# New orders of the TensorE, ScalarE and VectorE queues in the pair loop of a fused agent-attention and two-FFN kernel, with six of eight second-layer roundings on ScalarE

## Chip, cores and metric

The kernel runs on one NeuronCore of a Trainium2 chip. The metric is device time in microseconds (us), as the median over runs. Three runs of the kernel before took 1089.06, 1089.34 and 1089.91 us. The profiled execution is one further run.

## What is computed

The reference is an agent attention over 12480 tokens of width 128 with 49 agents, followed by two feed-forward layers of inner width 2048:

```python
a2k = sm(agents, k);  agent_v = a2k @ v
q2a = sm(q, agents);  x = q2a @ agent_v          # 12480 x 128
h = x @ w_in                                      # 12480 x 2048
g = where(h >= 1, h, where(h <= -1, 0, (h + 1)**2 / 4))
x = g @ w_out
h = x @ moe2_w_in
g = s * max(h, 0)**2 + b
out = g @ moe2_w_out
```

All of it is fp32. The weights of both layers arrive as 64-bit words and are decoded on the chip.

## The kernel before

A prologue computes `agent_v`, decodes the weights, and folds `agent_v` into the first layer's weights. A hand-written ramp then starts the first steps. From there on the function `steady()` runs to the end, and it is the part that matters here.

The tokens are cut into 25 tiles: the first of 256 columns, then 23 of 512, then one of 448. The inner width is cut into eight steps per tile, each of 256 rows (two blocks of 128), so there are 200 steps per layer. One step of a layer is a chain over the engines. In layer 1, for step n:

- H on TensorE makes the hidden block in PSUM; the two steps of a pair are made together by `H1_pair` (lines 720 and 726). Line 726 uses four quarters of the array at once.
- R and S on ScalarE are the two halves of the activation: a Relu out of PSUM (line 739) and a Square in place (line 745).
- M on VectorE caps the result (line 749) and is the last reader of that PSUM block.
- c on VectorE rounds it to `gh` (line 760), and L subtracts to get the remainder `gl` (line 765).
- O on TensorE multiplies by the output weights in six matmuls (line 804): for each of two blocks `gh` twice, then `gl`. The result is the tile `y`.

Layer 2 has the same chain in small letters: h (line 689, six matmuls), r (line 741), t (line 745), then the rounding, which is g: `G` on ScalarE (line 758) or `C` on VectorE (line 760), then l (line 765) and o (line 804, into the tile `o`). Layer 2 runs 11 steps behind layer 1. When a tile's eight steps are through, Y (line 823) and y (line 826) bring the first layer's result out of PSUM, and Z (line 830) brings out the second layer's as `osb`. The PSUM tiles `y` and `o` have one buffer each, so the first matmul of a tile waits for Y and y, or for Z, of the tile before. The hidden blocks h share three PSUM buffers, handed out in turn; `gh` and `gl` have four buffers per layer, x has three.

For later tiles the attention's softmax runs inside the same loop. Once in eight pairs of steps q (line 261) makes the scores of two tiles, Q (line 269) transposes them on VectorE, and twelve fillers F follow, one or two at a time; the last of them is a `spread` with a 1280-wide transposition (line 284), whose result 32 small DMAs take apart.

What sets the order: each engine works strictly through its own list, and the lists come from three strings in `PAIR`, used once per pair of steps n0, n0+1. A token is a letter and 0 or 1, for the step n0 or n0+1 (the small letters then mean the step 11 behind, or 12 and 13 behind for t, g, l and o). Tokens with nothing to do in a pair are skipped: Y, y and Z come up once in four pairs, q and Q once in eight. Which engine rounds is a pattern over the steps:

```python
def GH(layer, n):
    if layer == 1:
        return PAT1[n] if n < len(PAT1) else "0"
    return PAT2[n % len(PAT2)] if n < NS - TL else "0"
```

A "1" puts the rounding on ScalarE, a "0" on VectorE. The last steps run from the table `TAIL`.

Of the kernel before, what the change touches and what calls it, by code (L numbers as in the profile page):

```python
# [18 lines left out]
def kernel(  # L19
# [29 lines left out]
    Q1, QW, QG = 3, 256, 8  # L49

    GR, XB, UB, WB, KV = 4, 3, 4, 2, 7
    WARM, CD = 10, 1
    PAT1, PAT2, TL = "10011010001001", "11111101", 11

# [31 lines left out]
    PIECE = {"A0": (0, 512), "A2": (512, 512)}  # L88
    NR = 14
    PAIR = {  # L90
        "PE": "H0 h0 O0 o0 O1 h1 q1 o1".split(),
        "ACT": "t0 Y0 R0 R1 S0 S1 G0 r0 Y1 t1 r1 G1".split(),
        "DVE": "L0 y0 C0 C1 Z1 F0 M0 M1 l0 Z0 c0 y1 c1 L1 Q1 l1 F1".split(),
    }
    TAIL = {
        "PE": "H0 O0 h0 o0 O1 h1 o1".split(),
# [890 lines left out]
```

## Time and profile before

| | |
|---|---|
| median of three runs | 1089.34 us |
| the profiled execution's own time | 1089.8 us |
| its span, first to last instruction | 1088.0 us |
| TensorE busy | 1056.8 us, 97% of the span |
| VectorE busy | 961.4 us, 88% |
| ScalarE busy | 981.7 us, 90% |
| mean granted TensorE clock | 0.995 of full speed |

The busy time of an engine is the time that its instructions covered. For TensorE the ends of matmuls are modelled: a row of a matmul carries a duration that overlaps with the matmul after it, so the starts of two matmuls say more than the duration of one. A span of 1088.0 us and a time of 1089.8 us leave 1.8 us outside the profiled instructions. In the rows, PE is TensorE, PEld its weight load, DVE is VectorE, ACT is ScalarE.

### The profile page before, as it was taken

How to read it: one execution, taken by the hardware profiler on the slowest of the kernel's cores; microseconds unless marked ns; L12 is line 12 of the kernel's file. 1: busy time of each engine (PE TensorE's matmuls, PEld its weight loads, DVE VectorE, ACT ScalarE, POOL GpSimd, SP SyncE). 2: the span in 40 equal slices, each digit the busy share in tenths (PEclk: the TensorE clock that was granted, in tenths of full speed). 3: DMA queues.
4: the chain of work that ended last, by engine and by line, in shares of the span. 5: the costliest groups of instructions: out<-in, count | busy, mean ns of one | idle time of the engine just before them, and what ended most of it. 6: DMA issues, size and time to landing. Idle time of an engine off the chain costs nothing.

```text
span 1088.0 us, 13453 instructions
## 1 busy us (share of the span) xinstructions
PE 1056.8 (97%) x4962; PEld 793.3 (73%) x4962; DVE 961.4 (88%) x1114; ACT 981.7 (90%) x1101; POOL 0.9 (0%) x7
## 2 busy tenths in 40 slices
PE   6889989999999999999999999999999999999998
PEld 2667667777777777777777777777777777777777
DVE  8889979988988988988988988989989989988876
ACT  6889779999999999999999999999999999999986
POOL 0000000000000000000000000000000000000000
PEclk9899999999999999999999999999999999999999
DMA  9930020010020020020020020020020010010000
GB/s 349 395 103 29 21 63 10 17 53 10 13 57 11 12 57 11 11 57 10 12 57 10 11 59 10 10 59 10 8 60 11 9 41 11 9 38 10 1 11 19
DMA packets 32130, 47.68 MB, mean 44 GB/s; under 512 B 7301, under 2 KB 23669, under 8 KB 31425
## 3 DMA queue, kind: packets, MB, share of 16 engines
q1 hardware_dynamic: 32065, 46.83, 13.5%
q8 instruction: 39, 0.64, 0.3%
q14 instruction: 26, 0.21, 0.1%
HBM read 27.58 MB, written 6.39 MB: 31 GB/s over the span
## 4 chain that ended last, share of the span: by engine, by line
PE 74%; DVE 9%; ACT 8%; issue 4%; DMA 2%; SPq 2%; DVEq 0%; ACTq 0%
PE h L689 22%; PE o L804 22%; PE y L804 19%; PE h L720 6%; ACT x L739 3%; PE h L726 3%; DVE gl L765 3%; ACT x L745 3%; DVE x L749 2%; DMA wu<-in_w_out 2%; SPq L297 1%; ACT x L741 1%; DVE osb L830 1%; PE qs L261 1%; PE av L546 1%
## 5 line engine op out<-in xcount | busy, mean ns | idle before, releaser
L765 DVE TENSOR_TENSOR gl<-x,gh 128x1024 fp32r<-128x1024 f32 (+2 forms) x399 | 465.9, 1188 | 13.2 <-ACT gh L758 12.2
L745 ACT ACTIVATE x<-x 128x1024 f32<-128x1024 f32 (+2 forms) x399 | 403.2, 1039 | 2.6
L749 DVE SCALAR_TENSOR_TENSOR x<-h,x 128x1024 f32<-128x1024 f32 (+2 forms) x200 | 230.1, 1189 | 88.1 <-ACT x L745 88.0
L741 ACT ACTIVATE x<-h 128x1024 f32<-128x1024 f32 (+2 forms) x199 | 200.4, 1007 | 47.9 <-PE h L689 43.1
L739 ACT ACTIVATE x<-h 128x1024 f32<-128x1024 f32 (+2 forms) x200 | 190.1, 1002 | 18.8 <-PE h L726 16.7
L758 ACT ACTIVATE gh<-x 128x1024 fp32r<-128x1024 f32 (+1 forms) x172 | 176.7, 1029 | 1.1 <-DVE x L749 1.1
L689 PE MATMUL h<-yh,wi2h 128*128 128x512 f32 (+2 forms) x400 | 165.9, 415 | 5.1 <-DVE x L749 3.1
L804 PE MATMUL o<-gh,wo2h 128*128 128x512 f32 (+2 forms) x400 | 159.0, 398 | 3.8 <-DVE osb L830 2.7
L804 PE MATMUL y<-gl,wo1h 128*128 128x512 f32 (+2 forms) x400 | 156.4, 391 | 2.2 <-DVE gl L765 2.2
L804 PE MATMUL o<-gl,wo2h 128*128 128x512 f32 (+2 forms) x400 | 157.4, 393 | 0.6 <-DVE gl L765 0.4
L804 PE MATMUL y<-gh,wo1h 128*128 128x512 f32 (+2 forms) x400 | 155.9, 390 | 0.0
L804 PE MATMUL o<-gh,wo2l 128*128 128x512 f32 (+2 forms) x400 | 155.8, 390 | 0.0
L804 PE MATMUL y<-gh,wo1l 128*128 128x512 f32 (+2 forms) x400 | 155.7, 389 | 0.0
L689 PE MATMUL h<-yh,wi2l 128*128 128x512 f32 (+2 forms) x400 | 155.6, 389 | 0.0
L689 PE MATMUL h<-yl,wi2h 128*128 128x512 f32 (+2 forms) x400 | 155.5, 389 | 0.0
L760 DVE CAST gh<-x 128x1024 fp32r<-128x1024 f32 (+2 forms) x227 | 147.2, 674 | 6.8 <-ACT x L745 6.6
L689 PEld LDWEIGHTS h<-yh,wi2h 128*128 128x128 f32 x400 | 74.9, 187 | 42.8 <-issue 12.3
L720 PE MATMUL h<-pt,awm 128*128 128x512 f32 (+1 forms) x368 | 100.0, 394 | 0.0
L804 PEld LDWEIGHTS o<-gh,wo2h 128*128 128x128 f32 x400 | 75.2, 188 | 32.9 <-ACT x L745 12.0
L804 PEld LDWEIGHTS o<-gl,wo2h 128*128 128x128 f32 x400 | 75.3, 188 | 22.3 <-DVE gl L765 5.4
L804 PEld LDWEIGHTS y<-gl,wo1h 128*128 128x128 f32 x400 | 75.1, 188 | 21.3 <-DVE gl L765 4.5
L804 PEld LDWEIGHTS y<-gh,wo1h 128*128 128x128 f32 x400 | 75.1, 188 | 17.1
(127 smaller groups left out, 837.9 us busy)
## 6 DMA issues: line engine op xcount, KB each, us to landing
k<-in_kT SPq DMA_DIRECT2D x12, 512.0 KB, 11.4
v<-in_v_main SPq DMA_DIRECT2D x12, 512.0 KB, 10.1
out_T<-osb SPq DMA_DIRECT2D x23, 256.0 KB, 2.0
pt<-turned SPq DMA_DIRECT2D x172, 32.0 KB, 1.9
px<-turned SPq DMA_DIRECT2D x172, 32.0 KB, 1.8
qbuf<-in_qT SPq DMA_DIRECT2D x10, 512.0 KB, 3.8
wu<-in_w_in SPq DMA_DIRECT2D x4, 1024.0 KB, 12.0
wu<-in_w_out SPq DMA_DIRECT2D x3, 1024.0 KB
```

The costliest lines, as they stand in the source:

```text
L261: nc.tensor.matmul(out=sc[j * RG:(j + 1) * RG, g], lhsT=a64[:, g * RG:(g + 1) * RG], rhs=qbuf[:, c0:c0 + QW].rearrange("p (b x) -> p b x", ...
L689: nc.tensor.matmul(out=h[:, i, :w], lhsT=a[:, sl], rhs=r, start=(m == 0), stop=(m == len(ops) - 1))
L720: nc.tensor.matmul(out=out[g], lhsT=awm[:, c * P:(c + 1) * P], rhs=pt_t[t][:, :w], start=True, stop=False)
L726: nc.tensor.matmul(out=out[g], lhsT=awx[r, q], rhs=px_t[t][r, :w], start=False, stop=True)
L739: nc.scalar.activation(out=x, in_=h, func=ACTF.Relu, scale=0.5, bias=0.5)
L741: nc.scalar.activation(out=x, in_=h, func=ACTF.Relu)
L745: nc.scalar.activation(out=x, in_=x, func=ACTF.Square)
L749: nc.vector.scalar_tensor_tensor(out=x, in0=h, scalar=1.0, in1=x, op0=ALU.max, op1=ALU.min)
L758: nc.scalar.activation(out=a, in_=x, func=ACTF.Copy)
L760: nc.vector.tensor_copy(out=a, in_=x)
L765: nc.vector.tensor_tensor(out=b, in0=x, in1=a.bitcast(F32), op=ALU.subtract)
L804: nc.tensor.matmul(out=o[:, :w], lhsT=l[:, c, :], rhs=r[:, i, :w], start=(c == 0 and m == 0), stop=(c == KF - 1 and m == 2),)
```

## The change

Three strings and one pattern are replaced. No instruction is new in kind, and no buffer changes. Over the kernel, ScalarE has 24 instructions fewer and VectorE 24 more: the second-layer rounding of the steps with n mod 8 = 2.

```diff
     GR, XB, UB, WB, KV = 4, 3, 4, 2, 7
     WARM, CD = 10, 1
-    PAT1, PAT2, TL = "10011010001001", "11111101", 11
+    PAT1, PAT2, TL = "10011010001001", "11011101", 11
     PIECE = {"A0": (0, 512), "A2": (512, 512)}
     NR = 14
     PAIR = {
-        "PE": "H0 h0 O0 o0 O1 h1 q1 o1".split(),
-        "ACT": "t0 Y0 R0 R1 S0 S1 G0 r0 Y1 t1 r1 G1".split(),
-        "DVE": "L0 y0 C0 C1 Z1 F0 M0 M1 l0 Z0 c0 y1 c1 L1 Q1 l1 F1".split(),
+        "PE": "H0 O0 o0 h0 O1 h1 o1 q1".split(),
+        "ACT": "t0 R0 S0 G0 R1 S1 Y0 r0 Y1 t1 G1 r1".split(),
+        "DVE": "y0 Z1 C0 L0 C1 M0 F0 Z0 l0 c0 M1 y1 L1 l1 c1 Q1 F1".split(),
     }
     TAIL = {
         "PE": "H0 O0 h0 o0 O1 h1 o1".split(),
```

How this moves instructions is shown for one pair, n0 = 116. Names carry the layer and the step (`h1_116`, `gh2_104`, `x2_105`), then a running number; `y14` and `o12` carry the tile.

On TensorE, the first row of each block of the pair, before:

```order
L720 MATMUL h1_116_5537<-pt14_4756,awm_654 128x512 x2
...
L689 MATMUL h2_105_5547<-yh13_5383,wi2h_78 128x512
...
L804 MATMUL y14_5493<-gh1_114_5480,wo1h_76 128x512
...
L804 MATMUL o12_5240<-gh2_103_5530,wo2h_80 128x512
...
L804 MATMUL y14_5493<-gh1_115_5482,wo1h_76 128x512
...
L689 MATMUL h2_106_5596<-yh13_5383,wi2h_78 128x512
...
L804 MATMUL o13_5603<-gh2_104_5578,wo2h_80 128x512
```

and now:

```order
L720 MATMUL h1_116_5537<-pt14_4770,awm_654 128x512 x2
...
L804 MATMUL y14_5426<-gh1_114_5492,wo1h_76 128x512
...
L804 MATMUL o12_5245<-gh2_103_5526,wo2h_80 128x512
...
L689 MATMUL h2_105_5559<-yh13_5382,wi2h_78 128x512
...
L804 MATMUL y14_5426<-gh1_115_5533,wo1h_76 128x512
...
L689 MATMUL h2_106_5600<-yh13_5382,wi2h_78 128x512
...
L804 MATMUL o13_5607<-gh2_104_5575,wo2h_80 128x512
```

The block h0 (`h2_105`) has moved from ahead of both O0 and o0 to behind them, so that between the end of tile `o12` (its last block, on `gh2_103`) and the first block of `o13` there now lie three blocks in place of two. In pairs with q, its eight short matmuls stand behind o1 and no longer ahead of it.

On ScalarE, the pair n0 = 16 (the order is the same in every pair, but this one also has a Y, `yh1`, and the softmax's Exp, `turned`), before:

```order
L745 ACTIVATE x2_4_1105<-x2_4_1105 128x2x256
L306 ACTIVATE turned_653<-turned_653 128x8x49
L739 ACTIVATE x1_16_1155<-h1_16_1120 128x1024
L739 ACTIVATE x1_17_1157<-h1_17_1121 128x1024
L745 ACTIVATE x1_16_1155<-x1_16_1155 128x1024
L745 ACTIVATE x1_17_1157<-x1_17_1157 128x1024
L758 ACTIVATE gh2_4_1161<-x2_4_1105 128x2x256
L741 ACTIVATE x2_5_1163<-h2_5_1130 128x2x256
L823 ACTIVATE yh1_1165<-y1_892 128x512
L745 ACTIVATE x2_5_1163<-x2_5_1163 128x2x256
L741 ACTIVATE x2_6_1203<-h2_6_1180 128x2x256
L758 ACTIVATE gh2_5_1205<-x2_5_1163 128x2x256
```

and now:

```order
L745 ACTIVATE x2_4_1109<-x2_4_1109 128x2x256
L739 ACTIVATE x1_16_1154<-h1_16_1119 128x1024
L745 ACTIVATE x1_16_1154<-x1_16_1154 128x1024
L758 ACTIVATE gh2_4_1157<-x2_4_1109 128x2x256
L739 ACTIVATE x1_17_1159<-h1_17_1120 128x1024
L745 ACTIVATE x1_17_1159<-x1_17_1159 128x1024
L741 ACTIVATE x2_5_1162<-h2_5_1141 128x2x256
L823 ACTIVATE yh1_1164<-y1_892 128x512
L745 ACTIVATE x2_5_1162<-x2_5_1162 128x2x256
L758 ACTIVATE gh2_5_1168<-x2_5_1162 128x2x256
L306 ACTIVATE turned_653<-turned_653 128x8x49
L741 ACTIVATE x2_6_1222<-h2_6_1186 128x2x256
```

Each S now stands right behind the R whose result it reads, the rounding `gh2_4` comes two instructions earlier, and `gh2_5` right behind the Square that feeds it and ahead of the next r. The Exp, which waits for VectorE's softmax steps, stood ahead of this pair's R and now stands behind its G1.

On VectorE, the pair n0 = 116 again, before:

```order
L765 TENSOR_TENSOR gl1_115_5535<-x1_115_5428,gh1_115_5482 128x1024
L749 SCALAR_TENSOR_TENSOR x1_116_5572<-h1_116_5537,x1_116_5572 128x1024
L749 SCALAR_TENSOR_TENSOR x1_117_5574<-h1_117_5538,x1_117_5574 128x1024
L765 TENSOR_TENSOR gl2_104_5585<-x2_104_5528,gh2_104_5578 128x1024
L830 TENSOR_SCALAR osb12_5587<-o12_5240,s_sb_70,bcol_72 128x512
L760 CAST gh1_116_5590<-x1_116_5572 128x1024
L760 CAST gh1_117_5592<-x1_117_5574 128x1024
L765 TENSOR_TENSOR gl1_116_5594<-x1_116_5572,gh1_116_5590 128x1024
L765 TENSOR_TENSOR gl2_105_5633<-x2_105_5580,gh2_105_5622 128x1024
```

and now:

```order
L765 TENSOR_TENSOR gl1_115_5535<-x1_115_5445,gh1_115_5533 128x1024
L749 SCALAR_TENSOR_TENSOR x1_116_5572<-h1_116_5537,x1_116_5572 128x1024
L830 TENSOR_SCALAR osb12_5586<-o12_5245,s_sb_70,bcol_72 128x512
L765 TENSOR_TENSOR gl2_104_5589<-x2_104_5528,gh2_104_5575 128x1024
L760 CAST gh1_116_5591<-x1_116_5572 128x1024
L749 SCALAR_TENSOR_TENSOR x1_117_5577<-h1_117_5538,x1_117_5577 128x1024
L765 TENSOR_TENSOR gl1_116_5594<-x1_116_5572,gh1_116_5591 128x1024
L765 TENSOR_TENSOR gl2_105_5596<-x2_105_5580,gh2_105_5583 128x1024
L760 CAST gh1_117_5598<-x1_117_5577 128x1024
```

The second M (`x1_117`) has moved from right behind the first one to behind `osb`, l0 and c0, and so `osb12` has moved up past that M and past l0. A filler F0, where one is due, stood ahead of both M and now stands between the first M and Z0; the subtraction l1 (`gl2_105`) now precedes c1.

## Rows read from the trace of the kernel before

**Rows 1.** Busy us of each engine (and instructions) from 174.40 to 1011.63 us, clock, DMA.
```profile
174.40:1011.63 837.23, 834.11 (x3754) 625.69 (x3752) 753.33 (x824) 780.80 (x830) 0.00 (x0) 1.00 0.09 25
```

**Rows 2.** Timeline of TensorE: start and duration in us; L720 begins a pair.
```profile
613.61 1.09 PE L720 MATMUL h<-pt,awm 128*128 128x512 f32 x4
...
615.06 0.50 PE L689 MATMUL h<-yh,wi2h 128*128 128x512 f32 x1
...
623.83 1.08 PE L720 MATMUL h<-pt,awm 128*128 128x512 f32 x4
...
634.13 1.08 PE L720 MATMUL h<-pt,awm 128*128 128x512 f32 x4
...
645.28 1.08 PE L720 MATMUL h<-pt,awm 128*128 128x512 f32 x4
...
655.23 0.62 PE L720 MATMUL h<-pt,awm 128*128 128x512 f32 x2
```

**Rows 3.** Timeline of TensorE and VectorE around a first matmul of a tile o.
```profile
631.71 0.80 DVE L830 TENSOR_SCALAR osb<-o,s_sb,bcol 128x512 f32<-128x512 f32 x1
632.15 0.40 PE L689 MATMUL h<-yh,wi2l 128*128 128x512 f32 x1
...
632.66 0.48 PE L804 MATMUL o<-gh,wo2h 128*128 128x512 f32 x1
```

**Rows 4.** Timeline of the same two engines one pair earlier.
```profile
617.87 1.50 DVE L284 STREAM_TRANSPOSE turned<-packed 128x1280 f32<-128x1280 f32 x1
619.29 2.31 DVE L749 SCALAR_TENSOR_TENSOR x<-h,x 128x1024 f32<-128x1024 f32 x2
621.53 1.20 DVE L765 TENSOR_TENSOR gl<-x,gh 128x1024 fp32r<-128x1024 f32 x1
...
622.16 0.40 PE L804 MATMUL o<-gh,wo2h 128*128 128x512 f32 x1
...
622.39 0.39 PE L804 MATMUL o<-gh,wo2l 128*128 128x512 f32 x1
...
622.79 0.50 PE L804 MATMUL o<-gl,wo2h 128*128 128x512 f32 x1
```

**Rows 5.** Timeline of ScalarE in two pairs.
```profile
599.92 1.02 ACT L741 ACTIVATE x<-h 128x1024 f32<-128x1024 f32 x1
600.97 1.06 ACT L745 ACTIVATE x<-x 128x1024 f32<-128x1024 f32 x1
...
603.37 1.05 ACT L758 ACTIVATE gh<-x 128x1024 fp32r<-128x1024 f32 x1
604.32 1.05 ACT L745 ACTIVATE x<-x 128x1024 f32<-128x1024 f32 x1
```

**Rows 6.** Two of the page's costliest groups: busy us, mean ns of one.
```profile
L758 ACT ACTIVATE gh<-x 128x1024 fp32r<-128x1024 f32 (+1 forms) x172 | 176.7, 1029 | 1.1 <-DVE x L749 1.1
...
L760 DVE CAST gh<-x 128x1024 fp32r<-128x1024 f32 (+2 forms) x227 | 147.2, 674 | 6.8 <-ACT x L745 6.6
```

**Rows 7.** Timeline of two early pairs, n0 = 16 and n0 = 24, each to the next.
```profile
109.87 1.09 PE L720 MATMUL h<-pt,awm 128*128 128x512 f32 x4
...
113.48 0.55 ACT L306 ACTIVATE turned<-turned 128x392 f32<-128x392 f32 x1 [3.49 <-DVE turned L303]
...
118.10 0.39 PE L689 MATMUL h<-yh,wi2h 128*128 128x256 f32 x1 [1.81 <-DVE x L749]
...
120.85 1.80 PE L720 MATMUL h<-pt,awm 128*128 128x512 f32 x4
...
152.33 1.08 PE L720 MATMUL h<-pt,awm 128*128 128x512 f32 x4
...
156.53 0.54 ACT L306 ACTIVATE turned<-turned 128x392 f32<-128x392 f32 x1 [3.69 <-DVE turned L303]
...
164.45 1.08 PE L720 MATMUL h<-pt,awm 128*128 128x512 f32 x4
```

**Rows 8.** Busy us and granted clock (the first number after POOL's) of a short stretch.
```profile
118.90:122.50 3.60, 3.25 (x12) 2.29 (x10) 3.60 (x6) 2.37 (x5) 0.00 (x0) 0.53 0.00 0
```

## The prediction

> **What bounds the kernel now.** I read the stretch table first, because the page's average mixes a prologue with the loop. Between the first matmul of pair n0 = 28 (174.40 us) and that of n0 = 192 (1011.63 us) lie 82 pairs in 837.23 us, and TensorE is busy for 834.11 of them; ScalarE is busy 93% of the stretch, VectorE 90% [rows 1]. Read so, TensorE is full and there is nothing to win. The timeline says otherwise. Two matmuls of one block start 0.23 us apart, while each row claims 0.39 to 0.40 us [rows 4]: a row covers its successor's start, so a gap of up to 0.16 us does not show as idle. The measure to use is the time from one pair's first matmul to the next one's. It is 9.95 us in a pair with no wait (645.28 to 655.23). This is also the sum of its parts: H takes 1.45 (613.61 to 615.06), then six blocks of six matmuls at 0.23 make 8.4, and 0.1 is left for the change from quarter-array to full matmuls [rows 2, 4]. The other three pairs shown take 10.22, 10.30 and 11.15 us [rows 2]. The last one holds the eight score matmuls q, so q costs 1.20.
>
> The 10.30 is a wait for `osb`: a matmul due 0.23 after 632.15 starts at 632.66, because `osb` began at 631.71 and took 0.80 [rows 3]. The 10.22 is a wait for `gl`: the third matmul of an o block starts 0.40 after the second, when the subtraction that began at 621.53 has ended. That subtraction had stood behind the spread's transposition (1.50) and two caps (2.31) [rows 4]. So TensorE is the bound, and it loses time only where VectorE delivers late.
>
> A rule bears on this. The page Perfetto Trace Analysis of the Trainium skill (Identifying the Most-Contended Engine) says that the busy share of matmuls does not measure how near TensorE is to its limit. The trace agrees: by busy share 3.1 us of the stretch could be won, by start times three times that.
>
> **Term 1, the loop from n0 = 28 to 192.** With no wait left it would take 82 x 9.95 + 9 x 1.20 (nine pairs with q) = 826.7 us against 837.23: a gain of 10.5. Counted by waits: a tile ends in 21 of the pairs, at 0.35, and the spread falls in 10, at 0.27, together 10.1, so these two waits are the whole loss. The question is whether the new queues remove them and bring no other. I walk one pair by hand, from its first matmul at 0.
>
> TensorE: H 0, O0 1.45, o0 2.95, h0 4.35, O1 5.75, h1 7.15, o1 8.55, next pair 9.95.
>
> ScalarE: an instruction that reads its predecessor's result starts 0.03 after that one's end, so 1.05 after its start (599.92 to 600.97); one that doesn't starts 0.95 after it (603.37 to 604.32) [rows 5]. The new order makes R-S (twice), r0-t1 and r1-t0 pairs of the dear kind, and t1-G1 as well (1.09). With R0 at 1.65 (H's last matmuls end shortly after the next block begins): S0 2.70, G0 3.65, R1 4.60, S1 5.65, r0 6.60, t1 7.65, G1 8.74, r1 9.69, t0 10.74, R0 11.69. That is 10.04 per pair with G0 and 9.09 without. Half the pairs now have none, so the mean is 9.57; Y in one pair of four and the Exp in one of eight add about 0.2 (estimate: each half of a full instruction). ScalarE thus needs some 9.75 of 9.95: it fits, with 0.2 to spare.
>
> VectorE: M0 waits for S0, 2.70 + 1.06 + 0.03 = 3.79, and takes 1.16. `osb` follows directly: 4.95 to 5.75. The first matmul of the next tile wants it at 8.55; there were 0.1 to 0.3 too few, now there are 2.8 to spare. Then l0 6.95, c0 7.63, M1 8.79, L1 10.0, l1 11.2 (G1 is there at 9.82), c1 11.9, next L0 13.1, each time being an end. They are wanted: l0 at 9.02 (third matmul of o1), M1 at 9.95 (its PSUM buffer for the next H), c0 at 11.40, L1 at 11.87, l1 at 13.37. The least margin is 1.2, M1 before H. In the pair with the spread, 1.50 replaces `osb`: l0 ends at 7.65, which is 1.4 in time where it was late. M1 then ends at 9.5, and that pair also has a C0 in front (0.67), so M1 beats H by 0.4 at best. This spot I price from 0 to 0.4 us, ten times: 0 to 4.
>
> Moving 24 roundings costs VectorE 24 x 0.67 = 16 us and frees ScalarE of 24 x 1.03 = 25 [rows 6]. Both lie beside TensorE's work, VectorE going from 90 to about 92% of the stretch; without that cover the 16 would be on the path. I take 10.5 for the term. No wait is left to win beyond it, so that is its upper end; the lower end is a loss, which rival 3 prices.
>
> **Term 2, two early pairs.** Pair 16 takes 10.98 us (109.87 to 120.85) and pair 24 takes 12.12 (152.33 to 164.45). In both, ScalarE stands 3.49 and 3.69 us at the softmax's Exp, which waits for VectorE, with both R queued behind it; then h waits for a cap, 1.81 us at 118.10 [rows 7]. Now the Exp stands behind G1, at the end of a pair, and R0 starts when H is ready. In pair 16 four blocks work on the 256-column tile, 24 matmuls at half of 0.23, so TensorE needs only 7.2. ScalarE needs 2 x (1.05 + 0.95) for R and S, about 3.3 for six half-width instructions and 0.9 for Y and Exp, so 8.2, and that bounds it: a gain of 2.8. Pair 24 should come to 10.1, as h0, which shares its PSUM buffer with the softmax's scores, now stands 2.9 us later: a gain of 2.0. Together 4.8, with ends 0 (the stall returns at another instruction) and 7 (the neighbours gain too). For the pairs between and the end of the program I add 0.5.
>
> Part of pair 16's loss is the clock. From 118.90 to 122.50 the granted clock was 0.53 of full speed, mostly 1.2 GHz and not 2.4, right after the idle of 1.81 us [rows 7, 8]; (1 - 0.53) x 3.60 = 1.7 us. That it falls after idling is what the page TensorE: Matmul & The Clock Gate (HAM oscillation) says, and by it a shorter idle keeps the clock. The 2.8 counts this already.
>
> **Sum.** 1089.8 - 10.5 - 4.8 - 0.5 = 1074.0 for an execution like the profiled one; that one lay 0.46 above the median of 1089.34, so 1073.5.
>
> **Rivals.**
> 1. *Nothing to win.* TensorE's busy share is the truth and its starts are paced by something that no queue order moves: at most the 3.1 us of idle go [rows 1], so 1086 to 1089. Against it: the pair without a wait takes 9.95 and the ones with a named wait more.
> 2. *Half of it.* The thin spot (M1 before H after the spread) takes up to 4, or the early stall only changes place, with VectorE's transposition of the scores still waiting for the 32 DMAs: 1078 to 1086. For it: those DMAs aren't touched. Against: a margin of 0.4, and only pairs 22 to 24 are near the DMAs.
> 3. *Slower: ScalarE becomes the bound.* Place: the ring t0 to r1 in each pair. It fits by 0.2 us, and the new order puts five instructions behind their own producer. If each of these cost 0.04 more than rows 5 say, ScalarE paces the loop, and every further 0.1 per pair adds about 9 us over 90 pairs. It undoes the whole gain of 15.8 at 0.18 per pair beyond the fit, so 0.4 in all, 4% of the ring; at 6%, 1107 us. For it: ScalarE is already busy 93% [rows 1]. Against: the same R-S spacing of 1.05 is in the trace now, between r0 and t1.
> 4. *The change doesn't do what it says.* The order lists show 24 instructions changing sides and the blocks moved, so I give this nothing.
>
> **How the numbers follow.** The forecast (1070 to 1078) has 0.74, rival 2 has 0.15, rival 1 has 0.05, rival 3 has 0.06. The range from 1070.5 to 1081 leaves out rivals 1 and 3, about half of 2 and a little of the forecast's fast end, about 2 in 10. About 0.2% (2.2 us) is what can be told from no change: faster 0.90 (forecast, rival 2, a sliver of 1), same 0.04, slower 0.06.
>
> **What would show it.** Right: pairs at 9.95 throughout and 11.15 with q; `osb` ending some 2.8 us before its matmul; no line-749 wait behind Exp near pairs 16 and 24, and no stretch at half clock there; rows of line 741 to 758 at 1.09. Wrong: pairs of 10.0 to 10.4 with TensorE waiting for ScalarE (rival 3), H waiting for a cap once in eight pairs (rival 2), or pairs of 10.3 as before (rival 1). The sum goes wrong first in term 2, where neighbours in short pairs push each other, and in the hand walk if VectorE's starts drift late by more than 1.2 us.

## The result, and the profile after

The changed kernel took 1073.55 us (median of four runs, 1072.56 to 1073.93), the kernel before 1089.28 beside it. The ratio is 0.9853, with a 95% interval from 0.9836 to 0.9870. The forecast was 1073.5.

The profiled execution took 1073.31 us with a span of 1071.5. First its page: busy time and share of each engine, the chain that ended last, and three of the costliest groups (busy us, mean ns of one, idle time before them).

```profile
PE 1050.3 (98%) x4962; PEld 794.5 (74%) x4962; DVE 985.8 (92%) x1138; ACT 994.8 (93%) x1077; POOL 0.9 (0%) x7
...
PE 87%; DVE 5%; DMA 2%; ACT 2%; SPq 2%; issue 1%; DVEq 0%; ACTq 0%
...
L749 DVE SCALAR_TENSOR_TENSOR x<-h,x 128x1024 f32<-128x1024 f32 (+2 forms) x200 | 238.5, 1194 | 38.2 <-ACT x L745 37.9
...
L760 DVE CAST gh<-x 128x1024 fp32r<-128x1024 f32 (+2 forms) x251 | 169.8, 677 | 15.9 <-ACT x L745 15.2
...
L758 ACT ACTIVATE gh<-x 128x1024 fp32r<-128x1024 f32 (+1 forms) x148 | 151.8, 1027 | 4.1 <-DVE x L749 1.1
```

The 24 roundings have changed sides (148 and 251 in place of 172 and 227), and TensorE is now 87% of the chain (74% before). The same stretch as in [rows 1], from pair 28 to pair 192:

```profile
168.91:995.75 826.84, 826.84 (x3754) 628.10 (x3752) 776.20 (x846) 791.32 (x809) 0.00 (x0) 1.00 0.09 25
```

It takes 826.84 us, 10.39 less than before; the working gave 826.7. The same 3754 matmuls now count as 826.84 us busy and not 834.11: the busy time of before held 7.3 us of waiting, inside rows that reach past their successor's start. The rule of the Trainium skill cited in the prediction (Perfetto Trace Analysis, Identifying the Most-Contended Engine) says that this share is no good measure, since pipelined matmuls look smaller than they are. The trace agrees on the first; here the rows are too long and not too short.

Next, the timeline of the pairs n0 = 114 (with the spread's transposition, from 602.83) and 116 (a tile ends, from 612.78), cut to the rows that answer to [rows 2 to 4].

```profile
602.83 1.09 PE L720 MATMUL h<-pt,awm 128*128 128x512 f32 x4
...
608.17 1.50 DVE L284 STREAM_TRANSPOSE turned<-packed 128x1280 f32<-128x1280 f32 x1
...
609.59 1.18 DVE L765 TENSOR_TENSOR gl<-x,gh 128x1024 fp32r<-128x1024 f32 x1
...
611.29 1.22 DVE L749 SCALAR_TENSOR_TENSOR x<-h,x 128x1024 f32<-128x1024 f32 x1
...
611.85 0.39 PE L804 MATMUL o<-gl,wo2h 128*128 128x512 f32 x1
...
612.78 1.08 PE L720 MATMUL h<-pt,awm 128*128 128x512 f32 x4
...
616.56 1.22 DVE L749 SCALAR_TENSOR_TENSOR x<-h,x 128x1024 f32<-128x1024 f32 x1
...
617.70 0.80 DVE L830 TENSOR_SCALAR osb<-o,s_sb,bcol 128x512 f32<-128x512 f32 x1
...
620.15 1.22 DVE L749 SCALAR_TENSOR_TENSOR x<-h,x 128x1024 f32<-128x1024 f32 x1
...
620.36 1.06 ACT L745 ACTIVATE x<-x 128x1024 f32<-128x1024 f32 x1
...
621.34 0.39 PE L804 MATMUL o<-gh,wo2h 128*128 128x512 f32 x1
621.45 1.06 ACT L758 ACTIVATE gh<-x 128x1024 fp32r<-128x1024 f32 x1
...
622.74 0.62 PE L720 MATMUL h<-pt,awm 128*128 128x512 f32 x2
```

The pairs take 9.95 and 9.96 us. `osb` ends at 618.50, 2.84 ahead of its matmul at 621.34 (forecast 2.8). After the spread, l0 ends at 610.77, 1.08 ahead of the third o matmul (forecast 1.4 for that pair's walk), and the second cap at 612.51, 0.27 ahead of the next H (forecast 0.4 at best). The rounding behind its own Square starts 1.09 after it, as forecast. The pairs are the sign to go by: from 28 to 192 every pair takes 9.95 or 9.96 us, save the nine with q (11.04) and the nine behind them (10.05 or 10.06). The view of waits shows no wait of TensorE from 168.9 to 985 us, but of the 10.4 us lost before it showed only 1.8, as a short wait lies under the row before it.

The two early pairs, first as busy time and clock of pairs 16 and 18, then the timeline of pair 24 (they answer to [rows 7, 8]):

```profile
109.86:117.05 7.19, 7.19 (x48) 5.96 (x45) 7.02 (x10) 5.44 (x7) 0.00 (x0) 1.00 0.23 73
117.05:125.93 8.88, 8.56 (x46) 6.01 (x45) 8.81 (x15) 8.69 (x14) 0.00 (x0) 1.00 0.00 1
```

```profile
147.74 1.20 PE L720 MATMUL h<-pt,awm 128*128 128x512 f32 x4
...
151.81 0.72 DVE L269 STREAM_TRANSPOSE turned<-qs 128x512 f32<-128x512 f32 x1 [3.02 <-DMA pt<-turned]
...
152.58 0.50 PE L689 MATMUL h<-yh,wi2h 128*128 128x512 f32 x1 [0.22 <-DVE turned L269]
...
154.92 0.50 PE L804 MATMUL y<-gl,wo1h 128*128 128x512 f32 x1 [0.20 <-DVE gl L765]
...
158.96 1.09 PE L720 MATMUL h<-pt,awm 128*128 128x512 f32 x4
```

Pair 16 takes 7.19 us (forecast 8.2) with the clock at full speed; pair 24 takes 11.22 (forecast 10.1), because Q (line 269) waits 3.02 us for the spread's DMAs and h0 and a `gl` come late behind it.

Where the span's 16.5 us went: 10.39 from pair 28 to 192; 5.48 from pair 16 to 28 (64.53 to 59.05), of which pair 16 gave 3.79 and pair 24 0.90; 0.63 behind pair 192; nothing ahead of pair 16.

### The profile page after: what moved, and what is told of

The parts are those of the page before. It is cut to its first block, busy times and chain, and to the rows that moved or that the text cites. A ratio compares the mean times of both kernels' runs of the same rounds, so it can differ in the third digit from the quotient of the medians.

```text
span 1071.5 us, 13417 instructions
## 1 busy us (share of the span) xinstructions
PE 1050.3 (98%) x4962; PEld 794.5 (74%) x4962; DVE 985.8 (92%) x1138; ACT 994.8 (93%) x1077; POOL 0.9 (0%) x7
## 4 chain that ended last, share of the span: by engine, by line
PE 87%; DVE 5%; DMA 2%; ACT 2%; SPq 2%; issue 1%; DVEq 0%; ACTq 0%
PE y L804 24%; PE o L804 24%; PE h L689 24%; PE h L720 8%; PE h L726 4%; DMA k<-in_kT 2%; SPq L297 1%; DVE gl L765 1%; DVE x L749 1%; PE qs L261 1%; PE av L546 1%; ACT x L739 1%; ACT x L745 1%; DVE gh L760 1%; PE ks L492 0%
## 5 line engine op out<-in xcount | busy, mean ns | idle before, releaser
L765 DVE TENSOR_TENSOR gl<-x,gh 128x1024 fp32r<-128x1024 f32 (+2 forms) x399 | 471.9, 1191 | 10.1 <-ACT gh L758 6.6
L745 ACT ACTIVATE x<-x 128x1024 f32<-128x1024 f32 (+2 forms) x399 | 414.6, 1040 | 11.5
L749 DVE SCALAR_TENSOR_TENSOR x<-h,x 128x1024 f32<-128x1024 f32 (+2 forms) x200 | 238.5, 1194 | 38.2 <-ACT x L745 37.9
L739 ACT ACTIVATE x<-h 128x1024 f32<-128x1024 f32 (+2 forms) x200 | 198.2, 991 | 25.6 <-PE h L726 24.2
L741 ACT ACTIVATE x<-h 128x1024 f32<-128x1024 f32 (+2 forms) x199 | 197.4, 992 | 8.5 <-PE h L689 7.5
L760 DVE CAST gh<-x 128x1024 fp32r<-128x1024 f32 (+2 forms) x251 | 169.8, 677 | 15.9 <-ACT x L745 15.2
L804 PE MATMUL y<-gh,wo1h 128*128 128x512 f32 (+2 forms) x400 | 165.6, 414 | 0.0
L689 PE MATMUL h<-yh,wi2h 128*128 128x512 f32 (+2 forms) x400 | 156.2, 391 | 1.1 <-ACT x L741 0.9
L804 PE MATMUL o<-gh,wo2h 128*128 128x512 f32 (+2 forms) x400 | 155.8, 390 | 0.2 <-DVE osb L830 0.2
L758 ACT ACTIVATE gh<-x 128x1024 fp32r<-128x1024 f32 (+1 forms) x148 | 151.8, 1027 | 4.1 <-DVE x L749 1.1
L720 PE MATMUL h<-pt,awm 128*128 128x512 f32 (+1 forms) x368 | 101.0, 395 | 0.2 <-ACT x L741 0.2
```

Of the source, the lines that this page charges most:

```text
L689: nc.tensor.matmul(out=h[:, i, :w], lhsT=a[:, sl], rhs=r, start=(m == 0), stop=(m == len(ops) - 1))
L720: nc.tensor.matmul(out=out[g], lhsT=awm[:, c * P:(c + 1) * P], rhs=pt_t[t][:, :w], start=True, stop=False)
L739: nc.scalar.activation(out=x, in_=h, func=ACTF.Relu, scale=0.5, bias=0.5)
L741: nc.scalar.activation(out=x, in_=h, func=ACTF.Relu)
L745: nc.scalar.activation(out=x, in_=x, func=ACTF.Square)
L749: nc.vector.scalar_tensor_tensor(out=x, in0=h, scalar=1.0, in1=x, op0=ALU.max, op1=ALU.min)
```

## The experiments

All start from the kernel before or from the changed one, with the lines shown replaced. "Loop" is the time from pair 28 to pair 192.

### Each of the four edits alone

The pattern alone, then TensorE's, ScalarE's and VectorE's order alone:

```diff
-    PAT1, PAT2, TL = "10011010001001", "11111101", 11
+    PAT1, PAT2, TL = "10011010001001", "11011101", 11
```
```diff
-        "PE": "H0 h0 O0 o0 O1 h1 q1 o1".split(),
+        "PE": "H0 O0 o0 h0 O1 h1 o1 q1".split(),
```
```diff
-        "ACT": "t0 Y0 R0 R1 S0 S1 G0 r0 Y1 t1 r1 G1".split(),
+        "ACT": "t0 R0 S0 G0 R1 S1 Y0 r0 Y1 t1 G1 r1".split(),
```
```diff
-        "DVE": "L0 y0 C0 C1 Z1 F0 M0 M1 l0 Z0 c0 y1 c1 L1 Q1 l1 F1".split(),
+        "DVE": "y0 Z1 C0 L0 C1 M0 F0 Z0 l0 c0 M1 y1 L1 l1 c1 Q1 F1".split(),
```

> Only the rounding pattern is changed (six of eight on ScalarE); the three orders are as before. Theory (the gain comes from VectorE serving osb, l0 and c0 ahead of its second cap, and the pattern only makes ScalarE's new ring fit): with the old orders ScalarE was not what TensorE waited for, so 1087 to 1091 us, and the osb wait (0.35 us, 21 times) and the gl wait of before are still there. Rival (the 24 roundings taken off ScalarE are themselves the gain, since ScalarE was 93% busy): 1080 us or less.

> Only TensorE's order is changed (h0 behind o0, q behind o1). Theory: the first matmul of the next layer-2 tile stands 8.55 us after the pair's start in both orders, and osb is not made any earlier, so the osb wait stays: 1087 to 1091 us. Rival (the extra block between the end of one tile and the start of the next gives osb one block, 1.4 us, more time): the osb wait goes, 7 us less, 1080 to 1083 us.

> Only ScalarE's order is changed (R0 S0 G0 R1 S1 with seven of eight roundings still on ScalarE). Theory: VectorE's old order has both caps in a row ahead of l0 and osb, so M1 now waits for S1, about 1 to 2 us later than before, and all behind it (l0, osb, c0) comes later by as much; ScalarE's ring is also above 9.95 in seven of eight steps: slower, 1110 to 1130 us, with a longer osb wait (over 1 us). Rival (ScalarE's order alone lets the first cap start early and is a gain in itself): 1080 to 1087 us.

> Only VectorE's order is changed. Theory: osb and l0 now stand ahead of M1, so their waits go (up to 10 us), but S0 comes as late as before behind R0 R1, and M1 now stands behind osb, l0 and c0, so H waits for M1 and gives most of it back: 1083 to 1090 us, with the osb wait gone and a wait of H for line 749 in its place. Rival (VectorE's order alone is the whole gain): 1073 to 1078 us.

Measured, with the ratio to the kernel before (1089.44 us):

| edit alone | us | ratio, 95% interval |
|---|---|---|
| pattern | 1089.18 | 0.9997 [0.9988, 1.0007] |
| TensorE's order | 1089.11 | 1.0001 [0.9991, 1.0010] |
| ScalarE's order | 1129.46 | 1.0369 [1.0353, 1.0384] |
| VectorE's order | 1084.01 | 0.9950 [0.9933, 0.9966] |

The first two do nothing alone, as the theory had it. ScalarE's order alone costs 40 us, as its theory had it (1110 to 1130). Three of its waits from 168 to 985 us (us in total, times, longest):

```profile
DVE x L749 <- ACT x L745: 108.8, 95, 1.7
...
PE o L804 <- DVE osb L830: 22.2, 19, 1.2
...
PE o L804 <- DVE gl L765: 7.3, 9, 0.9
```

VectorE, with both caps in a row, now waits for the later S1, and `osb` behind them comes so late that TensorE stands idle for up to 1.2 us at each tile's end; `gl` is late as well, once behind each spread.

VectorE's order alone brings only 5 of the 16 us. The theory's time holds, but its reason does not: no wait of H for line 749 is there. The loop takes 832.88, 6 us over the changed kernel's, and all of it lies in the pair after each q. From the timeline there:

```profile
642.21 1.08 PE L720 MATMUL h<-pt,awm 128*128 128x512 f32 x4
...
643.56 0.71 DVE L269 STREAM_TRANSPOSE turned<-qs 128x512 f32<-128x512 f32 x1
...
644.32 0.50 PE L689 MATMUL h<-yh,wi2h 128*128 128x512 f32 x1 [0.59 <-DVE turned L269]
```

Q now stands last in VectorE's order, the scores hold a PSUM buffer until Q has read them, and h0, right behind H in TensorE's old order, waits for that buffer: 10.61 us in place of 9.95, nine times, 5.9 in all. Pair 24, where Q is late because of the DMAs, takes 15.68, with a granted clock of 0.78 in it.

### Which orders are needed together

Everything but TensorE's order; VectorE's and TensorE's orders without ScalarE's and the pattern; the three orders with the old pattern; and the three orders with all eight roundings on ScalarE. For the last, the diff is

```diff
-    PAT1, PAT2, TL = "10011010001001", "11111101", 11
+    PAT1, PAT2, TL = "10011010001001", "11111111", 11
```

The others are made of the lines above.

> The whole change but TensorE's order (h0 stays ahead of O0 and o0). In the changed kernel the score transposition Q ends 0.86 us after its pair's start (634.64 against 633.78); h0 of the old order would want its buffer 1.45 after the start, so it should just fit. Theory (VectorE's and ScalarE's orders carry the gain; TensorE's is needed only where Q comes late): 1073 to 1077 us, the pairs from 28 on at 9.95, and any loss in the pair at about 150 us, where Q waits for the DMAs. Rival (h0 behind o0 is what shields every pair after q, as the 0.66 us wait for line 269 nine times with VectorE's order alone suggests): 1078 to 1082 us with pairs of 10.6.

> VectorE's and TensorE's new orders, ScalarE's order and the pattern as before. Theory of the hand walk (M1 stands late, so S0 must be early, which only the R0 S0 G0 R1 S1 order gives): H waits for M1 in many pairs, 1078 to 1083 us. Rival (ScalarE's order is not needed: with VectorE's order alone no osb, gl or H wait was left, only h0's wait for Q, 0.66 us nine times and about 4 us once near 160 us, and h0 behind o0 takes these away): 1072 to 1076 us, as the whole change.

> The three new orders with the old pattern (seven of eight second-layer roundings on ScalarE). Theory (ScalarE's ring is 10.04 us in a pair with G0, so three in four pairs are just over 9.95, and the slack is taken up by the pair without): 1074 to 1077 us. Rival (the pattern is what makes the new orders fit at all): over 1080 us, with TensorE waiting for ScalarE or for M1.

> The three new orders with all eight roundings on ScalarE, to measure how near ScalarE is to the bound. By the hand walk each pair then costs ScalarE 10.04 us and about 0.2 for Y and Exp, 10.24 in the mean against TensorE's 9.95 and 10.08 with q: ScalarE paces the loop at about 10.2, so 82 pairs cost 10 to 14 us more than with six: 1083 to 1088 us, with pairs of 10.0 to 10.5. Rival (ScalarE's real ring is shorter than the hand walk, as dependent instructions are dear only where nothing stands between): 1073 to 1077 us.

Measured beside 1089.73 us of the kernel before:

| kernel | us | ratio, 95% interval | loop |
|---|---|---|---|
| all but TensorE's order | 1077.61 | 0.9889 [0.9874, 0.9904] | 827.50 |
| VectorE's and TensorE's | 1074.18 | 0.9857 [0.9843, 0.9872] | 826.85 |
| three orders, seven of eight | 1073.42 | 0.9855 [0.9839, 0.9872] | 826.95 |
| three orders, eight of eight | 1087.49 | 0.9980 [0.9971, 0.9990] | 837.37 |

Without TensorE's order nearly all of the loss is in pair 24, 15.90 us against 11.22; the pairs after q are at 9.95, and the loop loses 0.7, as one pair in eight takes 10.02. So the theory's mechanism holds, at 0.6 us more than its range, and the rival's 10.6 does not come back. Pair 24, and the busy time and clock of the stretch behind its wait:

```profile
147.51 1.08 PE L720 MATMUL h<-pt,awm 128*128 128x512 f32 x4
...
151.43 0.72 DVE L269 STREAM_TRANSPOSE turned<-qs 128x512 f32<-128x512 f32 x1 [3.00 <-DMA pt<-turned]
...
152.21 0.80 PE L689 MATMUL h<-yh,wi2h 128*128 128x512 f32 x1 [3.18 <-DVE turned L269]
152.80 0.63 PE L689 MATMUL h<-yl,wi2h 128*128 128x512 f32 x1
153.23 0.63 PE L689 MATMUL h<-yh,wi2l 128*128 128x512 f32 x1
```
```profile
152.21:157.92 5.71, 5.71 (x14) 4.46 (x14) 5.67 (x7) 2.93 (x3) 0.00 (x0) 0.50 0.47 139
```

Q comes 3.92 us after the pair's start, much as in the changed kernel (4.07); h0 stands earlier and waits 3.18 us for it and not 0.22. The wait is not the whole price: behind it the granted clock is 0.50, 1.2 GHz, for 5.7 us, and two matmuls start 0.43 us apart and not 0.23. Of the 5.95 us that this pair takes beyond 9.95, 3.25 are the late start of h0 (152.21 in place of 148.96), and some 2.5 the lower clock (the 15 starts behind it, to 158.28, take 6.07 us in place of 3.6). In the changed kernel the short wait of pair 24 leaves the clock at 1.00.

With VectorE's and TensorE's orders alone the whole gain is there: 0.9857 against 0.9853 for the whole change, so what ScalarE's order and the pattern add can't be told from nothing in the times; in the traces it is 1.1 us between pairs 16 and 28 (60.19 against 59.05), and nothing in the loop. This is the run where the theory of the hand walk fell (it expected 1078 to 1083). Its timeline at the walk's thin spot, the end of the pair with the spread, and in the tile-end pair behind it:

```profile
612.39 1.21 DVE L749 SCALAR_TENSOR_TENSOR x<-h,x 128x1024 f32<-128x1024 f32 x1
...
613.04 1.09 PE L720 MATMUL h<-pt,awm 128*128 128x512 f32 x4
614.06 0.51 PE L726 MATMUL h<-px,awx 19*128 19x512 f32 x4
...
618.78 0.80 DVE L830 TENSOR_SCALAR osb<-o,s_sb,bcol 128x512 f32<-128x512 f32 x1
...
621.60 0.40 PE L804 MATMUL o<-gh,wo2h 128*128 128x512 f32 x1
```

The second cap ends at 613.60, 0.56 after the next H has begun, and H waits for nothing: its second line follows after 1.02, as in pairs with no wait. The walk took the three PSUM buffers to go round in strict turn, which gives the cap's buffer to the next H. The traces don't bear this out, nor the "handed out in turn" of the section on the kernel before. In this kernel the semaphores that both blocks of H wait for there are ScalarE's alone, so the cap's buffer goes to a later block. In the changed kernel the first block waits for ScalarE too, and the second, which starts 0.46 us behind it, for VectorE. And `osb`, behind a first cap that comes 0.8 later than with ScalarE's new order, still ends at 619.58, 2.02 ahead of its matmul.

Seven of eight costs nothing against six (826.95 and 826.84 in the loop; 1073.42 us is 0.6 under its theory's range); eight of eight costs 10.5 there. Its stretch table from pair 28 to 192, then H behind the spread in pair 68 and the cap ahead of it:

```profile
169.62:1006.99 837.37, 834.43 (x3754) 625.88 (x3752) 752.88 (x804) 823.35 (x849) 0.00 (x0) 1.00 0.09 25
```
```profile
372.66 1.22 DVE L749 SCALAR_TENSOR_TENSOR x<-h,x 128x1024 f32<-128x1024 f32 x1
...
373.23 1.43 PE L720 MATMUL h<-pt,awm 128*128 128x512 f32 x4
374.59 0.51 PE L726 MATMUL h<-px,awx 19*128 19x512 f32 x4
```

ScalarE is busy 98% of it, and eight pairs (301.61 to 383.53) take 81.92 us, 10.24 in the mean, where TensorE alone needs 10.10 (8 x 9.95 and one q). The hand walk's ring of 10.04 plus its estimate of 0.2 for Y and Exp is 10.24. So the theory holds, and rival 3's bound is real: it begins between seven and eight roundings, not at six. The loss is not spread over the eight: four take 9.95 or 9.96, and the pair with the spread (10.25), the tile's end (10.30) and the pair behind q (10.52) carry it. One of these places is the walk's thin spot: the cap, behind a late ScalarE, ends at 373.88, and line 726 follows 1.36 behind the start of H in place of 1.02, as the second block had to wait for the buffer.

### The one move that carries the loop

```diff
-        "DVE": "L0 y0 C0 C1 Z1 F0 M0 M1 l0 Z0 c0 y1 c1 L1 Q1 l1 F1".split(),
+        "DVE": "L0 y0 C0 C1 Z1 F0 M0 l0 Z0 c0 M1 y1 c1 L1 Q1 l1 F1".split(),
```

And, for pair 24, the DMAs that take the spread apart: they are collected in a list and sorted, so that for the second tile (j > 1) the ones that read the columns of `turned` that the next Q overwrites (c = 0 and 1, which go to `pt`) stand ahead of its others.

```diff
-                for dst, main in ((pt_t[t], True), (px_t[t], False)):
-                    for c in range(4):
-                        nc.sync.dma_start(
...
+                        todo.append((j > 1 and not (main and c < 2), dst, main, c, x0, n, src))
+            todo.sort(key=lambda d: d[0])
+            for _, dst, main, c, x0, n, src in todo:
+                nc.sync.dma_start(
```

The DMA order was run with the one move, and with the whole change beside the change itself.

> The kernel before with one thing changed: in VectorE's order M1 goes from right behind M0 to behind l0, Z0 and c0; all else (TensorE, ScalarE, pattern, the rest of VectorE) as before. Theory (what gained is that osb and l0 no longer stand behind the second cap): the osb and gl waits go, 10 us; Q1 stays ahead of l1, so h0 waits less for it than the 0.66 us with the whole new VectorE order; the pair near 150 us keeps its DMA wait: 1075 to 1081 us, loop pairs of 9.95. Rival (the rest of the new VectorE order, C0 and L0 behind Z1 and the filler behind M0, is needed too): 1083 to 1090 us, with new waits for M1 or gl.

> The run with only M1 moved, and the spread's 32 DMAs in another order: the two columns that the next transposition Q overwrites go first for the second tile. Theory (near 150 us Q waits for those DMAs, and with TensorE's old order h0 stands right behind H and waits for Q): that pair goes from 12 to 16 us down to 10 to 11.5, so 2 to 5 us less than with M1 moved alone. Rival (the pair is held by something else): the same time as with M1 moved alone, within 0.1%.

> The whole change, and the spread's 32 DMAs in the new order. Theory: Q no longer waits 3.02 us at 151.81, h0 and gl of that pair are in time, and the pair of 11.21 us takes 10.0: 1.2 us less than the change alone, 1072.3 us. Rival (the wait only moves, to the matmuls that read the spread's later columns): 1073.5 us or more, with TensorE waiting for a DMA of pt or px near 148 us.

> The changed kernel itself, on the same chip as the runs beside it: 1073.5 us, within 0.1% of the first measurement; it is the base for the DMA order.

Measured beside 1089.23 us of the kernel before:

| kernel | us | ratio, 95% interval | loop | pair 16 | pair 24 |
|---|---|---|---|---|---|
| M1 moved | 1080.53 | 0.9918 [0.9904, 0.9931] | 827.54 | 10.96 | 13.21 |
| M1 moved, DMAs | 1078.65 | 0.9902 [0.9888, 0.9915] | 827.66 | 10.19 | 10.44 |
| the change, DMAs | 1071.93 | 0.9840 [0.9827, 0.9853] | 826.83 | 7.19 | 10.06 |
| the change again | 1072.48 | 0.9853 [0.9839, 0.9866] | 826.83 | 7.28 | 11.20 |

Moving one token gives 9.7 of the loop's 10.4 us, with every other token of all three engines where it was. In this kernel's pair with a tile's end:

```profile
618.92 1.09 PE L720 MATMUL h<-pt,awm 128*128 128x512 f32 x4
...
623.53 1.22 DVE L749 SCALAR_TENSOR_TENSOR x<-h,x 128x1024 f32<-128x1024 f32 x1
...
626.48 0.80 DVE L830 TENSOR_SCALAR osb<-o,s_sb,bcol 128x512 f32<-128x512 f32 x1
...
627.47 0.43 PE L804 MATMUL o<-gh,wo2h 128*128 128x512 f32 x1
```

The pair's start plus 8.55 is 627.47, so the first matmul of the new tile comes when it is due, with `osb` done at 627.28, only 0.19 ahead (2.84 in the changed kernel). In most such pairs a loss of 0.03 to 0.05 is left. The early pairs are not cured by the move: 16 stays at 10.96, and 24 is 1.1 us longer than before, with a granted clock of 0.87 in it.

With the DMAs reordered, pair 24 goes from 13.21 to 10.44 beside the one move (1.9 us in the whole, just under the 2 to 5 expected; with the shorter wait the clock of this pair is 1.00 and not 0.87, which is part of the 2.77), and from 11.20 to 10.06 in the changed kernel. In these two kernels the same lines have numbers higher by 4 from there on, so line 724 is H:

```profile
147.28 1.20 PE L724 MATMUL h<-pt,awm 128*128 128x512 f32 x4
148.23 0.72 DVE L269 STREAM_TRANSPOSE turned<-qs 128x512 f32<-128x512 f32 x1
...
157.33 1.09 PE L724 MATMUL h<-pt,awm 128*128 128x512 f32 x4
```

Q starts 0.95 after the pair and waits for no DMA, against 4.07 in the changed kernel. The theory holds in the trace: 1.14 us in that one pair. In whole times the version is 0.55 us ahead of the change (medians), the intervals overlap, and the change itself came out 1.07 lower here than in its first measurement, so that it is faster than the change is shown by the pair and not by the times. It is faster than the kernel before by 1.6%.

## Why the prediction was right, point by point

**What bounds the kernel.** Right. TensorE's start times were the measure: the loop went to 82 pairs at 9.95 and nine q at 1.20 (11.04 and 10.06 for a q pair and its follower, in place of 11.15 and 9.95), and nothing was left beside TensorE.

**Term 1.** 10.39 against 10.5. The two waits named, `osb` and `gl`, were the loss, and the one move of M1 takes nearly all of both. The hand walk's times for the changed kernel held to 0.3 us in what was compared (`osb`, l0, the second cap). Two things in it were wrong without moving the sum. Its thin spot, M1 before H after the spread, priced from 0 to 4 us, was set against the wrong matmul: in the changed kernel the block that waits for VectorE starts 0.46 after H, so the margin is 0.73 and not 0.27; with seven roundings M1 ends 0.02 after H's start and nothing is lost. In the run without ScalarE's order it ends 0.56 after and nothing is lost either, as that H does not take M1's buffer. Only with eight roundings (0.65 after) does the spot cost anything, some 0.2 us a time. And the walk leaned on an early S0 as much as on the moved cap. With ScalarE's old order `osb` is still 2.0 early: the moved cap did it, and ScalarE's early S0 adds a margin that no wait needs.

**The move of 24 roundings** was costed at nothing, hidden beside TensorE. Right: the pattern alone measures 0.9997, and the three orders run as fast with the old pattern. What it could have protected, ScalarE's fit, holds with seven of eight as well.

**TensorE's order** had no term of its own in the loop, and alone it gives nothing. But the working did not see what it is for: VectorE's new order puts Q last, and without h0 behind o0 that costs 5.9 us in the loop with ScalarE's old order (0.7 with the new one) and 4.5 to 4.7 in pair 24, of which some 2.5 are the lower clock. Two edits of which one is worth 5 alone and the other nothing are worth 15.6 together.

**Term 2** was mis-sized in both parts, and the errors cancelled: 4.69 against 4.8.
- *Pair 16* gained 3.79, not 2.8. The step that failed was "so 8.2, and that bounds it": ScalarE's work of a pair need not be done within that pair. ScalarE was busy 5.44 us of pair 16's 7.19 and 8.69 of the next pair's 8.88, and TensorE's own 7.2 became the bound. And the Exp stands behind G1 by VectorE's order, in which F0, the filler that issues it, stands behind the first M and no longer ahead of it; ScalarE's order doesn't move it. With ScalarE's order alone it is still ahead of R0 and waits as long as before (3.54 us), and the pair takes 11.56. VectorE's order alone brings the pair to 8.57, and both with the pattern to 7.13.
- *Pair 24* gained 0.90, not 2.0. The step that failed was that h0, 2.9 us later, is clear of Q. Q itself came 4.07 after the pair's start, held by the DMAs, and h0 started at 152.58. It was due 0.23 behind the row at 151.97, so it is 0.38 late, of which its row shows 0.22 as idle; the `gl` at 154.92 is 0.37 late in the same way, and behind each the next matmul starts 0.33 or 0.34 later and not 0.23. Reordering the DMAs gives the 1.14 back. This is the second leg of rival 2, at a quarter of the price that this rival began with.

**The clock** was mis-sized. Before, it was granted at 0.53 from 118.90 to 122.50, behind an idle of 1.81 us [rows 7, 8]; after, there is no such idle, and 1.00 in pairs 16 and 18. The rule of the Trainium skill cited there (TensorE: Matmul & The Clock Gate, HAM oscillation) says that the clock falls after idling; that trace agrees. But the run with the pattern alone has the same idle and keeps its clock. Its matmul behind the idle, then its pairs 16 and 18:

```profile
116.55 0.39 PE L689 MATMUL h<-yh,wi2h 128*128 128x256 f32 x1 [1.81 <-DVE x L749]
```
```profile
108.31:118.85 10.54, 7.72 (x46) 5.88 (x45) 8.27 (x12) 6.92 (x11) 0.00 (x0) 1.00 0.17 50
118.85:128.11 9.26, 8.43 (x46) 6.25 (x45) 9.19 (x15) 7.43 (x11) 0.00 (x0) 1.00 0.00 1
```

So this idle does not bring the clock down every time, and where it did, less was lost than the 1.7 us that the prediction works out: pairs 16 and 18 together take 19.80 us here at full clock against 19.84 before (10.98 and 8.86), as pair 18 is shorter where 16 is longer. The two kernels with M1 moved part in the same way: 19.90 with the clock down (0.92 and 0.90), 19.45 with the same idle and the DMAs in the new order at 1.00. That is 0.04 and 0.45 us, from single executions of kernels that differ in one more thing each.

**The 0.5 for the rest** was small: pairs 18, 20, 22 and 26 gave 0.79 and the end 0.63. That is why the profiled execution lies 0.7 under the sum's 1074.0; the median was hit because the two profiled executions lay on different sides of their medians, by 0.46 above and 0.24 below. That it came within 0.1 us is luck, in this and in term 2; the loop's 10.39 is not.

**Rivals.** Rival 1 fell with the loop. Of rival 2, the thin spot cost nothing and the DMAs 1.1 us. Rival 3's mechanism was shown by the run with eight roundings, at the price that the walk gives; with six it has at least the room of one more rounding in eight steps, since seven run as fast.

## What to carry to other kernels

In an engine's own list, put the result that the bottleneck waits for ahead of work with slack: here one cap moved behind `osb`, l0 and c0 was worth 9.7 of 10.4 us in the loop. Before calling an edit useless because it gives nothing alone, look for what another edit delays: TensorE's order was worth nothing beside VectorE's old order and 10 us beside VectorE's new one. And in a pipelined loop, hold an engine's work against several pairs, not one: only what is over in the mean becomes a bound.

## What the runs showed that was not expected

- A wait of TensorE is larger than its row says: 0.38 us of delay stood as 0.22 of idle at 152.58, and 0.1 more was lost at the matmul behind it.
- A wait of 3.18 us cost TensorE nearly twice its length: the clock granted behind it was 0.50 for 5.7 us (pair 24 without TensorE's order).
- With ScalarE as the pacing engine, the time is the sum of its list: 10.24 us in the mean of eight pairs, and 10.24 from the spacings of 0.95, 1.05 and 1.09 with the estimate of 0.2 for Y and Exp.
- The 32 small DMAs of a spread take about 20 us of SyncE's queue, at some 0.62 us each (four in 2.49 us); it is their order, not their bytes, that held VectorE for 3 us.
